# Attention with two feed-forward layers: the maxima's row as one DMA from SBUF into q's stack, and copies merged into fewer DMAs

## The chip, the cores and the metric

The kernel runs on one core of a Trainium2 chip. The metric is the device time of one execution in microseconds (us); smaller is better. TensorE (PE) does matrix products, VectorE (DVE), ScalarE (ACT) and GpSimd (POOL) the rest, SyncE (SP) issues nearly all DMAs.

## The reference

```python
def _attn_ref(q, k, v, g_q, g_k):              # q, k, v: (4, 12, 448, 64) float32
    q_n, k_n = (rmsnorm(q, g_q), rmsnorm(k, g_k))
    scores = scale * np.matmul(q_n, k_n.transpose(0, 1, 3, 2))
    scores = scores - np.max(scores, axis=-1, keepdims=True)
    attn = np.exp(scores)
    attn = attn / (np.sum(attn, axis=-1, keepdims=True) + 1e-09)
    return np.matmul(attn, v)
...
def _moe_ref(x, w_in, w_out, g_ln):            # x: (1792, 768), d_ff 1024
    h = x @ w_in
    solu = h * softmax(h)
    return (layer_norm(solu) * g_ln) @ w_out
...
def _moe2_ref(x, w_in, w_out):                 # d_ff 2048
    h = x @ w_in
    return ((h - np.tanh(h)) @ w_out)
```

The weights of the two layers come as 64-bit floats.

## The kernel before

Products are made more exact than one pass by splitting each operand into a high part and a rest; a product is then three passes (`three`, L174).

There are 4 batches of 12 heads. Heads are taken two at a time: 24 pairs. For each pair the kernel loads q and k (`load_qk`), normalises them (`norm`), transposes them on TensorE (`qk_trans`, twice), and splits them: ScalarE writes the high part, VectorE the rest. For every pair but the first, DMAs then copy these parts from a work tile (`wq`, `wk`) into stacks `Q` and `K`. A stack holds 128 partitions, so that one pass over it multiplies two parts at a time: for one head, the high part of q lies in 64 partitions and its rest in the other 64 (slot z = 0); slot z = 1 has the high part again, and in the other 64 partitions zeros, but for one partition, into which the row of that head's negated maxima is written. k's stack has ones opposite that row, so the pass subtracts the maximum of each query from its scores.

The row is made thus. `maxima` multiplies q's and k's high parts and VectorE takes the maximum of each query (`nm`, L355). `spread` transposes 4 columns of `nm` on TensorE (L362), ScalarE copies the 4x128 result to `nt` (L364), and two DMAs of SyncE's queue carry it: `nt` to a scratch tensor `m` in HBM (L367), and from there to the row in `Q` (L370). `weights` then makes the scores with the stacks (`sps`, L393), ScalarE the exponentials (`pf`, L404), and `pv` multiplies with v (`pvps`, L440 and L446). `load_v` fetches v: two DMAs of 3x128 rows, and one of 64 rows for the last 64 keys of each head (its tail).

The list `attn` gives each of these steps a slot; `spread` of a pair's first head comes 3 steps ahead of the first `weights` that needs its row, `spread` of its second head 2 steps ahead of the tail that needs it. After the first batch the steps are laid between those of the first feed-forward layer of the batch before (`overlap`: `moe_h`, `layer_norm`, `moe_x2`), and weights are fetched (L114), split (L153), saved to HBM (L157) and read again (L167) beside it. From 560 us on only the second layer is left.

The order on each engine isn't the code's: a planner lays the instructions by costs of its own when the program is built, and each engine then runs its list in order. SyncE's DMAs are one such list: an instruction that waits holds all behind it. Each DMA tells of its landing by one of eight semaphores, which the DMAs take in turn as the planner laid them, and it isn't issued before the one that had that semaphore last has landed.

Of the kernel before, what the change touches and what calls it, by code (L numbers as in the profile page):

```python
# [8 lines left out]
F32 = mybir.dt.float32  # L9
F32R = mybir.dt.float32r  # L10
# [8 lines left out]
def kernel(  # L19
# [14 lines left out]
    nc = tc.nc  # L34
    B, H, S, D = q.shape
# [7 lines left out]
    CP = S // 4  # L43
# [10 lines left out]
    NQ = 3  # L54
# [5 lines left out]
    dram = ctx.enter_context(tc.tile_pool(name="dram", bufs=1, space=bass.MemoryType.DRAM))  # L60
# [142 lines left out]
    def load_v(p):  # L203
        b, h = pair(p)
        if p in V32:

            t = vhl_t[p] = A["vh"].tile([128, 14, D], F32, tag="va", name="v32")
            tv = t.rearrange("p (a z) d -> p a z d", z=2)
            nc.gpsimd.memset(tv[:, :, 1], 1.0)
            for i in range(2):  # L210
                r = slice(64 * i, 64 * i + 64)
                nc.sync.dma_start(
                    out=tv[:, 3 * i:3 * i + 3, 0],
                    in_=v[b, h + i, 0:384, :].rearrange("(c p) d -> p c d", p=128),
                )
                nc.sync.dma_start(out=tv[r, 6, 0], in_=v[b, h + i, 384:448, :])
            return
        t = A["v"].tile([128, 7, D], F32, tag="v", name="vraw")
# [64 lines left out]
    def qk_trans(p, a):  # L283

        ps = ps_m.tile([128, 4, CP], F32, tag="m", name="qkps")
        for c in range(4):
            nc.tensor.transpose(ps[:, c], qn_t[p][:, a, c].rearrange("p h d -> p (h d)"), idf[:CP, :CP])
        if a == 0:
            w = Q[0][:, 0] if p == 0 else A["one"].tile([128, 2, 4, CP], F32R, tag="wq", name="wq")
            split(w[:, 0], w[:, 1], ps)  # L290
        else:
            w = K[0][:, 0] if p == 0 else A["one"].tile([128, 2, S], F32R, tag="wk", name="wk")
            hi, lo = (w[:, z].rearrange("r (p c) -> r p c", c=4) for z in range(2))
            pv = ps.rearrange("r c p -> r p c")
            nc.scalar.activation(out=hi, in_=pv, func=AF.Copy, scale=gam)
            nc.vector.scalar_tensor_tensor(
                out=lo, in0=pv, scalar=gam, in1=hi.bitcast(F32), op0=ALU.mult, op1=ALU.subtract,
            )
        w_t[p, a] = w
        if a == 0:  # L300
            for i in range(2):
                r = slice(64 * i, 64 * i + 64)
                f = 384 * (1 - i)
                copy(
                    nc.scalar, out=qd[p % 2][r, r],
                    in_=w[r, 0].rearrange("p c q -> p (c q)")[:, f:f + 64].bitcast(F32),
                )
        if p == 0:
            return

        t = Q[p % 2] if a == 0 else K[p % NQ]
        for i in range(2):
            r, o = slice(64 * i, 64 * i + 64), slice(64 - 64 * i, 128 - 64 * i)
# [18 lines left out]
    def fill_q(z):  # L332
        for i in range(2):
            o = slice(64 - 64 * i, 128 - 64 * i)
            constant(Q[z][o, i, 1].rearrange("p c q -> p (c q)"), o, zero)

    def maxima(p, c):


        if p not in nm_t:  # L340
            nm_t[p] = A["small"].tile([128, 7], F32, tag="nm", name="nm")
        ps = ps_x.tile([128, S], F32, tag="x", name="mps")
        i = c // 4
        r = slice(64 * i, 64 * i + 64)
        if c == 3:
            nc.tensor.matmul(ps, lhsT=qd[p % 2], rhs=w_t[p, 1][:, 0], start=True, stop=True)
        else:
            if p == 0:
                qh, kh = w_t[0, 0][r, 0], w_t[0, 1][r, 0]
            else:  # L350

                qh, kh = Q[p % 2][:, i, 0], K[p % NQ][:, i, 0]
            f = 128 * c if i == 0 else 128 * (c - 4) + 64
            nc.tensor.matmul(ps, lhsT=qh.rearrange("p c q -> p (c q)")[:, f:f + 128], rhs=kh, start=True, stop=True)  # L354
        nc.vector.tensor_reduce(out=nm_t[p][:, c:c + 1], in_=ps, axis=AX.X, op=ALU.max, negate=True)  # L355

    def spread(n):

        p, i = divmod(n, 2)
        o = 64 * i if p == 0 else 64 - 64 * i  # L360
        ps = ps_m.tile([128, 128], F32, tag="m", name="nmps")
        nc.tensor.transpose(ps[:4], nm_t[p][:, 3 * i:3 * i + 4], idf)  # L362
        nt = A["small"].tile([4, 128], F32R, tag="nt", name="nt")
        nc.scalar.activation(out=nt, in_=ps[:4], func=AF.Copy)  # L364
        t = (Q[0][o:o + 1, 1, i] if p == 0 else Q[p % 2][o:o + 1, i, 1]).rearrange("p c q -> p (c q)")
        m = dram.tile([4, 128], F32, name=f"m_{n}")
        nc.sync.dma_start(out=m, in_=nt.bitcast(F32))  # L367

        row = m.rearrange("(o c) q -> o (c q)", o=1)[:, 64 * i:64 * i + S]
        nc.sync.dma_start(out=t.bitcast(F32), in_=row)  # L370

    def weights(n, j):

# [2 lines left out]
        for i in ((1, 0) if j == 3 else (n % 2,)):  # L376
            r = slice(64 * i, 64 * i + 64)

            k0, m = ((384, 64), (320, 128))[i] if j == 3 else (128 * j, 128)
            if p == 0 and j == 3 and i == 0:  # L380

                p1, ps = ps, ps_x.tile([128, 4, CP], F32, tag="x", name="sps")
            o = ps[:m]
            if p == 0:
                qh, ql = w_t[0, 0][r, 0], w_t[0, 0][r, 1]
                kh, kl = w_t[0, 1][r, 0, k0:k0 + m], w_t[0, 1][r, 1, k0:k0 + m]
                nc.tensor.matmul(o, lhsT=kh, rhs=qh, start=True, stop=False)
                nc.tensor.matmul(o, lhsT=kh, rhs=ql, start=False, stop=False)
                nc.tensor.matmul(o, lhsT=kl, rhs=qh, start=False, stop=False)
                nc.tensor.matmul(o, lhsT=K[1][r, 1 - i, 1, :m], rhs=Q[0][r, 1, i], start=False, stop=True)  # L390
            else:
                for z in range(2):
                    nc.tensor.matmul(  # L393
                        o, lhsT=K[p % NQ][:, i, z, k0:k0 + m], rhs=Q[p % 2][:, i, z], start=(z == 0), stop=(z == 1)
                    )
        tail = "t" if j == 3 else ""
        x = A["pc" + tail if p in V32 else "pf"].tile(
# [315 lines left out]
    Q += [A["qt"].tile([128, 2, 2, 4, CP], F32R, tag=f"q{z}", name=f"q{z}") for z in range(2)]  # L713
    for z in range(2):
        o = slice(64 * z, 64 * z + 64)
        constant(Q[0][o, 1, z].rearrange("p c q -> p (c q)"), o, zero)
# [21 lines left out]
    b = 0  # L738
# [147 lines left out]
```

## Time and profile before

| | |
|---|---|
| time, median of 3 runs | 1158.94 us (1152.77 to 1166.38) |
| the profiled execution | 1158.77 us, of which the profile's span is 1156.9 us |
| TensorE busy | 1071.2 us (93%) |
| VectorE busy | 740.8 us (64%) |
| ScalarE busy | 525.3 us (45%) |
| DMA, share of 16 engines | 50.2% |

Busy time is that in which an engine executes; waits and DMA issues are not in it. A wait is put down to what ended it. The granted clock is TensorE's, as a share of 2.4 GHz: 0.50 is 1.2 GHz. Times inside the profile count from the span's start.

### The profile page before, as it was taken

Reading aid. Unit: us, or ns where it says so; the run is one execution under the profiler, and the core shown is the slowest. Engines: PE = TensorE matmul, PEld = TensorE weight load, DVE = VectorE, ACT = ScalarE, POOL = GpSimd, SP = SyncE. Lnnn points to the kernel's source line nnn. Section 1 sums busy time; section 2 is a strip of 40 time slices with the busy share of each in tenths; the row PEclk is TensorE's granted clock in tenths of the full one; section 3 lists DMA queues with packets and bytes.
Section 4 is the critical chain, followed back from the end, with each engine's and each line's share of the span. In section 5 each row is a group of like instructions: output and inputs, shape, how many; then the busy total and the mean of one; then the engine's idle time right before and its main releaser. Section 6 shows DMA issues by size and latency. Waiting matters only on the chain.

```text
span 1156.9 us, 19235 instructions
## 1 busy us (share of the span) xinstructions
PE 1071.2 (93%) x7152; PEld 948.0 (82%) x7152; DVE 740.8 (64%) x1331; ACT 525.3 (45%) x1064; POOL 263.5 (23%) x228
## 2 busy tenths in 40 slices
PE   5989988969887989997999999999999999999998
PEld 3545566646776779776998999999999999999998
DVE  8566677699798866654527045558575757667434
ACT  5466666688676767665226145312121212122111
POOL 3211122222312411111201031416050414142100
PEclk9999999998999899998999999999999999999999
DMA  6776688776997877765737534112121111211022
GB/s 173 204 220 170 169 220 230 217 216 208 266 290 239 251 207 212 194 210 165 247 110 227 181 125 137 60 52 74 38 74 38 56 56 46 65 37 56 1 83 110
DMA packets 112893, 171.53 MB, mean 148 GB/s; under 512 B 33328, under 2 KB 79136, under 8 KB 112800
## 3 DMA queue, kind: packets, MB, share of 16 engines
q1 hardware_dynamic: 112800, 170.30, 50.2%
q8 instruction: 57, 0.93, 0.3%
q14 instruction: 36, 0.29, 0.1%
HBM read 109.41 MB, written 29.20 MB: 120 GB/s over the span
## 4 chain that ended last, share of the span: by engine, by line
PE 66%; DMA 15%; DVE 9%; ACT 5%; issue 2%; SPq 1%; POOL 0%; DVEq 0%; ACTq 0%; POOLq 0%
PE ops L177 7%; PE h2ps L176 7%; PE h2ps L175 7%; PE h2ps L177 7%; PE ops L176 7%; PE ops L175 7%; PE pvps L440 5%; PE sps L393 3%; PE hps L175 2%; DMA w<-w_in 2%; DMA raw<-in_moe_w_out_dram 2%; PE x2ps L175 2%; PE hps L177 2%; PE hps L176 2%; PE x2ps L177 2%; PE x2ps L176 2%
## 5 line engine op out<-in xcount | busy, mean ns | idle before, releaser
L175 PE MATMUL ops<-w,gT 128*128 128x256 f32 x672 | 189.6, 282 | 1.4 <-ACT ob L818 0.8
L176 PE MATMUL h2ps<-x2s,w 128*128 128x256 f32 x672 | 189.5, 282 | 0.0
L176 PE MATMUL ops<-w,gT 128*128 128x256 f32 x672 | 189.4, 282 | 0.0
L177 PE MATMUL ops<-w,gT 128*128 128x256 f32 x672 | 188.9, 283 | 0.5 <-DVE gT L181 0.5
L177 PE MATMUL h2ps<-x2s,w 128*128 128x256 f32 x672 | 189.3, 282 | 0.0
L175 PE MATMUL h2ps<-x2s,w 128*128 128x256 f32 x672 | 189.3, 282 | 0.0
L154 POOL TENSOR_TENSOR w<-val,w 128x512 fp32r<-128x512 f32 x60 | 80.5, 1351 | 388.2 <-ACT w L153 382.1
L355 DVE TENSOR_REDUCE nm<-mps 128x1 f32<-128x448 f32 x168 | 103.1, 619 | 79.7 <-PE mps L354 73.7
L393 PE MATMUL sps<-q,k 128*128 128x448 f32 (+1 forms) x368 | 120.0, 415 | 23.0 <-DVE nm L355 9.4
L175 PEld LDWEIGHTS ops<-w,gT 128*128 128x128 f32 x672 | 127.7, 190 | 2.0 <-ACT ob L818 1.2
L176 PEld LDWEIGHTS ops<-w,gT 128*128 128x128 f32 x672 | 127.6, 190 | 0.0
L177 PEld LDWEIGHTS ops<-w,gT 128*128 128x128 f32 x672 | 126.8, 189 | 0.7 <-DVE gT L181 0.7
L175 PEld LDWEIGHTS h2ps<-x2s,w 128*128 128x128 f32 x672 | 127.2, 189 | 0.1
L177 PEld LDWEIGHTS h2ps<-x2s,w 128*128 128x128 f32 x672 | 127.0, 189 | 0.0
L176 PEld LDWEIGHTS h2ps<-x2s,w 128*128 128x128 f32 x672 | 126.9, 189 | 0.0
L798 DVE TENSOR_TENSOR th<-h2ps,th 128x512 f32<-128x512 f32 x56 | 38.6, 689 | 134.4 <-ACT th L797 134.4
L820 DVE TENSOR_TENSOR ob<-ops,ob 128x512 f32<-128x512 f32 x147 | 100.4, 687 | 24.5 <-PE ops L177 20.2
L797 ACT ACTIVATE th<-h2ps 128x512 f32<-128x512 f32 x56 | 33.4, 596 | 171.9 <-PE h2ps L177 171.3
L404 ACT ACTIVATE pf<-sps 128x448 f32<-128x448 f32 x167 | 87.6, 539 | 50.5 <-PE sps L393 42.5
L393 PEld LDWEIGHTS sps<-q,k 128*128 128x128 f32 (+1 forms) x368 | 63.5, 187 | 55.3 <-DVE nm L355 16.6
L175 PE MATMUL hps<-w,xs 128*128 128x256 f32 x336 | 97.4, 291 | 6.2 <-DMA w<-w_in 5.7
L176 PE MATMUL hps<-w,xs 128*128 128x256 f32 x336 | 95.9, 286 | 0.0
(139 smaller groups left out, 2371.2 us busy)
## 6 DMA issues: line engine op xcount, KB each, us to landing
w<-w_out SPq DMA_DIRECT2D x48, 512.0 KB
raw<-in_moe_w_in_dram SPq DMA_DIRECT2D x36, 512.0 KB
raw<-in_moe_w_out_dram SPq DMA_DIRECT2D x36, 512.0 KB
w<-w_in SPq DMA_DIRECT2D x36, 512.0 KB
q<-wq SPq DMA_DIRECT2D x138, 112.0 KB
k<-wk SPq DMA_DIRECT2D x46, 224.0 KB
w_in<-w SPq DMA_DIRECT2D x12, 512.0 KB
w_out<-w SPq DMA_DIRECT2D x12, 512.0 KB
```

The lines of the kernel that those rows point to most:

```text
L154: nc.gpsimd.tensor_tensor(out=w[:, 1], in0=x, in1=w[:, 0].bitcast(F32), op=ALU.subtract)
L175: nc.tensor.matmul(ps, lhsT=a[0], rhs=w[0], start=first, stop=False)
L176: nc.tensor.matmul(ps, lhsT=a[0], rhs=w[1], start=False, stop=False)
L177: nc.tensor.matmul(ps, lhsT=a[1], rhs=w[0], start=False, stop=last)
L355: nc.vector.tensor_reduce(out=nm_t[p][:, c:c + 1], in_=ps, axis=AX.X, op=ALU.max, negate=True)
L393: nc.tensor.matmul(o, lhsT=K[p % NQ][:, i, z, k0:k0 + m], rhs=Q[p % 2][:, i, z], start=(z == 0), stop=(z == 1))
L404: nc.scalar.activation(out=x, in_=ps, func=AF.Exp)
L440: nc.tensor.matmul(o, lhsT=w, rhs=x, start=first, stop=last)
L797: nc.scalar.activation(out=th, in_=ps, func=AF.Tanh)
L798: nc.vector.tensor_tensor(out=th, in0=ps, in1=th, op=ALU.subtract)
L820: nc.vector.tensor_tensor(out=o, in0=ps, in1=o, op=ALU.add)
```

## The change

The row no longer goes through HBM: one DMA, issued by ScalarE right behind its copy to `nt`, writes the 4x128 block into one partition of `Q`. The block is 64 elements longer than the row, so `Q` is laid out flat, with a gap of 64 that takes what is over. Because in that layout the two slots with q's high part lie side by side, the two DMAs that copied it become one, with a source that is read twice. The tails of v's two heads come in one DMA of 128 partitions instead of two of 64. At the start, four DMAs for the norms' factors become two; they and the layer norm's factor are issued by ScalarE.

```diff
+    QW, GAP = 4 * S + 64, 64
+    QO = {(0, 0): 0, (0, 1): S, (1, 1): 2 * S + GAP, (1, 0): 3 * S + GAP}
+    def qcols(t, o, p, i, z):
+        c = (2 + i) * S + GAP if p == 0 else QO[i, z]
+        return t[o, c:c + S]
...
     def load_v(p):
...
         for i in range(2):
             nc.sync.dma_start(
-                out=t[:, 3 * i:3 * i + 3],
+                out=chunks[:, 3 * i:3 * i + 3],
                 in_=v[b, h + i, 0:384, :].rearrange("(c p) d -> p c d", p=128),
             )
-            nc.sync.dma_start(out=t[64 * i:64 * i + 64, 6], in_=v[b, h + i, 384:448, :])
-        v_t[p] = t
+        nc.sync.dma_start(out=tails, in_=v[b, h:h + 2, 384:448, :])
...
     def qk_trans(p, a):
...
             if a == 0:
-                for z in range(2):
-                    nc.sync.dma_start(out=t[r, i, z].bitcast(F32), in_=w[r, 0].bitcast(F32))
-                nc.sync.dma_start(out=t[o, i, 0].bitcast(F32), in_=w[r, 1].bitcast(F32))
+                wf = w.rearrange("r z c q -> r z (c q)").bitcast(F32)
+                c = min(QO[i, 0], QO[i, 1])
+                nc.sync.dma_start(
+                    out=t[r, c:c + 2 * S].rearrange("r (z f) -> r z f", z=2).bitcast(F32),
+                    in_=wf[r, 0:1].to_broadcast([64, 2, S]),
+                )
+                nc.sync.dma_start(out=qcols(t, o, p, i, 0).bitcast(F32), in_=wf[r, 1])
...
     def spread(n):
...
         nc.scalar.activation(out=nt, in_=ps[:4], func=AF.Copy)
-        t = (Q[0][o:o + 1, 1, i] if p == 0 else Q[p % 2][o:o + 1, i, 1]).rearrange("p c q -> p (c q)")
-        m = dram.tile([4, 128], F32, name=f"m_{n}")
-        nc.sync.dma_start(out=m, in_=nt.bitcast(F32))
-        row = m.rearrange("(o c) q -> o (c q)", o=1)[:, 64 * i:64 * i + S]
-        nc.sync.dma_start(out=t.bitcast(F32), in_=row)
+        c = ((2 + i) * S + GAP if p == 0 else QO[i, 1]) - GAP * i
+        nc.scalar.dma_start(out=Q[p % 2][o:o + 1, c:c + S + GAP].bitcast(F32), in_=nt.bitcast(F32))
...
-    for z in range(2):
-        nc.sync.dma_start(out=gam[64 * z:64 * z + 64], in_=g_q.rearrange("(d o) -> d o", o=1))
-        nc.sync.dma_start(out=gam2[64 * z:64 * z + 64], in_=g_k.rearrange("(d o) -> d o", o=1))
-    nc.sync.dma_start(out=gln, in_=moe_g_ln.rearrange("(c p) -> p c", p=128))
+    for t, g in ((gam, g_q), (gam2, g_k)):
+        nc.scalar.dma_start(out=t, in_=g.rearrange("(o d) -> o d", o=1).to_broadcast([2, D]))
+    nc.scalar.dma_start(out=gln, in_=moe_g_ln.rearrange("(c p) -> p c", p=128))
```

SyncE's list in the first batch, where the copies of one pair into `k_164` and `q_166` stand. Before:

```order
L472 DMA xd<-xo 128x448
L320 DMA k_164<-wk 64x448
L319 DMA k_164<-wk 64x896
L370 DMA q_167<-m_709 1x448
L319 DMA k_164<-wk 64x896
L320 DMA k_164<-wk 64x448
L316 DMA q_166<-wq 64x448 x2
L317 DMA q_166<-wq 64x448
L316 DMA q_166<-wq 64x448 x2
L317 DMA q_166<-wq 64x448
L367 DMA m_804<-nt 4x128
```

The same copies on SyncE in the changed kernel, whose lines are some 8 higher:

```order
L480 DMA xd<-xo 128x448
L331 DMA k_164<-wk 64x448 x2
L330 DMA k_164<-wk 64x896 x2
L324 DMA q_166<-wq 64x2x448
L328 DMA q_166<-wq 64x448
L324 DMA q_166<-wq 64x2x448
L328 DMA q_166<-wq 64x448
```

The row's second DMA (L370) stood among the copies, and the next row's first (L367) behind them; now SyncE's list has neither, and six copies of q are four. In all SyncE issues 569 DMAs where it issued 740.

ScalarE's list at the same place, from one row's `nt` to the next. Before:

```order
L364 ACTIVATE nt<-nmps 4x128
L404 ACTIVATE pf<-sps 128x448
L295 ACTIVATE wk<-qkps,gam 128x448
L180 ACTIVATE wq<-qkps 128x448
L247 ACTIVATE sq<-qk 112x1024
L404 ACTIVATE pf<-sps 128x448
L74 ACTIVATE qd_160<-wq 64x64 x2
L128 ACTIVATE val<-raw_1497 128x512
L404 ACTIVATE pf<-sps 128x448
L364 ACTIVATE nt<-nmps 4x128
L404 ACTIVATE pf<-sps 128x448
```

The same on ScalarE in the changed kernel:

```order
L375 ACTIVATE nt<-nmps 4x128
L378 DMA q_166<-nt 1x4x128
L412 ACTIVATE pf<-sps 128x448
L302 ACTIVATE wk<-qkps,gam 128x448
L180 ACTIVATE wq<-qkps 128x448
L251 ACTIVATE sq<-qk 112x1024
L412 ACTIVATE pf<-sps 128x448
L74 ACTIVATE qd_160<-wq 64x64 x2
L412 ACTIVATE pf<-sps 128x448 x2
L375 ACTIVATE nt<-nmps 4x128
L378 DMA q_166<-nt 1x4x128
L466 ACTIVATE sx<-pvps,tiny 64x448
```

The row's DMA now stands right behind `nt`, ahead of the exponentials (`pf`) and of the copies of the transposed k and q (`wk`, `wq`); elsewhere in the list one to seven other instructions stand between.

## Rows read from the trace of the kernel before

**Rows 1.** Windows: stretch, length, busy us of PE, PEld, DVE, ACT, POOL, clock, DMA share, GB/s.

```profile
30.00:160.00 130.00, 117.91 (x456) 71.27 (x454) 79.94 (x155) 85.74 (x186) 26.89 (x30) 0.97 0.72 191
160.00:300.00 140.00, 119.12 (x593) 85.31 (x591) 117.78 (x232) 101.74 (x221) 36.91 (x35) 0.94 0.79 220
300.00:430.00 130.00, 109.83 (x581) 92.06 (x581) 105.93 (x213) 93.82 (x206) 31.14 (x29) 0.92 0.89 261
430.00:560.00 130.00, 116.99 (x696) 103.91 (x696) 78.35 (x145) 82.34 (x167) 22.30 (x23) 0.96 0.66 195
560.00:1157.00 597.00, 589.39 (x4792) 585.68 (x4791) 334.17 (x523) 146.55 (x250) 135.72 (x94) 1.00 0.27 86
```

**Rows 2.** Waits of PE in 0 to 560 us: total us, times, longest.

```profile
PE mps L354 <- DMA q<-wq: 9.8, 6, 3.2
PE sps L393 <- DVE nm L355: 9.4, 11, 1.7
PE sps L393 <- DMA q<-m: 8.6, 7, 3.5
...
PE mps L346 <- ACT qd L74: 4.7, 5, 1.9
PE sps L393 <- ACT pf L404: 4.6, 5, 1.8
...
PE mps L354 <- ACT pf L404: 2.8, 4, 1.1
PE sps L390 <- DMA q<-m: 1.9, 1, 1.9
```

**Rows 3.** Waits of SyncE's queue over the whole span.

```profile
SPq L370 <- DMA m<-nt: 31.1, 27, 4.2
SPq L367 <- ACT nt L364: 31.0, 19, 4.0
...
SPq L316 <- DMA raw<-in_moe_w_out_dram: 2.6, 2, 2.4
```

**Rows 4.** The page's chain that ended last, by engine.

```profile
PE 66%; DMA 15%; DVE 9%; ACT 5%; issue 2%; SPq 1%; POOL 0%; DVEq 0%; ACTq 0%; POOLq 0%
```

**Rows 5.** Timeline, 73 to 85 us: start, duration, instruction, idle before it and what ended it.

```profile
73.22 0.27 SPq L367 DMA_DIRECT2D m<-nt  x1
...
75.26 1.15 SPq L319 DMA_DIRECT2D k<-wk  x1
...
77.31 0.26 SPq L370 DMA_DIRECT2D q<-m  x1
...
79.46 2.12 SPq L316 DMA_DIRECT2D q<-wq  x2
...
81.02 0.67 PE L393 MATMUL sps<-q,k 128*128 128x448 f32 x2 [0.37 <-DMA q<-m]
...
84.92 0.44 PE L354 MATMUL mps<-k,q 128*128 128x448 f32 x1 [3.23 <-DMA q<-wq]
```

**Rows 6.** Single lines' DMA issues: ns least/median/most, first and last start.

```profile
L367 SPq DMA_DIRECT2D m<-nt x48: 265/293/674, 17.1 to 511.7; - x48
L370 SPq DMA_DIRECT2D q<-m x48: 218/242/440, 22.3 to 513.1; - x48
L316 SPq DMA_DIRECT2D q<-wq x92: 461/587/1524, 19.6 to 488.2; - x92
L718 SPq DMA_DIRECT2D gam<-in_g_q_dram x2: 568/582/596, 1.7 to 2.9; - x2
```

**Rows 7.** Windows with half the clock, first and last of six.

```profile
85.50:88.90 3.40, 2.82 (x6) 1.87 (x7) 1.15 (x2) 1.01 (x2) 0.00 (x0) 0.50 0.36 77
...
423.40:426.80 3.40, 3.40 (x11) 2.55 (x10) 1.25 (x3) 3.28 (x7) 0.00 (x0) 0.50 0.71 225
```

**Rows 8.** DMA queue of the page: packets, MB, share of 16 engines' span.

```profile
q1 hardware_dynamic: 112800, 170.30, 50.2%
```

More of the change, by code (lines that the diff above doesn't have):

```diff
@@ L209, in load_v @@
             nc.gpsimd.memset(tv[:, :, 1], 1.0)
[L210 to L218, printed above, removed]
+            chunks, tails = tv[:, 0:6, 0], tv[:, 6, 0]
+        else:
+            t = v_t[p] = A["v"].tile([128, 7, D], F32, tag="v", name="vraw")
+            chunks, tails = t[:, 0:6], t[:, 6]
         for i in range(2):
             nc.sync.dma_start(
-                out=t[:, 3 * i:3 * i + 3],
+                out=chunks[:, 3 * i:3 * i + 3],
                 in_=v[b, h + i, 0:384, :].rearrange("(c p) d -> p c d", p=128),
             )
-            nc.sync.dma_start(out=t[64 * i:64 * i + 64, 6], in_=v[b, h + i, 384:448, :])
-        v_t[p] = t
+        nc.sync.dma_start(out=tails, in_=v[b, h:h + 2, 384:448, :])
     def rsqrt(y, x, scale):
@@ L288, in qk_trans @@
         if a == 0:
-            w = Q[0][:, 0] if p == 0 else A["one"].tile([128, 2, 4, CP], F32R, tag="wq", name="wq")
+            w = (
+                Q[0][:, 0:2 * S].rearrange("r (z c q) -> r z c q", z=2, c=4) if p == 0
+                else A["one"].tile([128, 2, 4, CP], F32R, tag="wq", name="wq")
+            )
             split(w[:, 0], w[:, 1], ps)
@@ L314, in qk_trans @@
             if a == 0:
-                for z in range(2):
-                    nc.sync.dma_start(out=t[r, i, z].bitcast(F32), in_=w[r, 0].bitcast(F32))
-                nc.sync.dma_start(out=t[o, i, 0].bitcast(F32), in_=w[r, 1].bitcast(F32))
+                wf = w.rearrange("r z c q -> r z (c q)").bitcast(F32)
[3 more added lines that the diff above has]
+                    in_=wf[r, 0:1].to_broadcast([64, 2, S]),
+                )
+                nc.sync.dma_start(out=qcols(t, o, p, i, 0).bitcast(F32), in_=wf[r, 1])
             else:
@@ L334, in fill_q @@
             o = slice(64 - 64 * i, 128 - 64 * i)
-            constant(Q[z][o, i, 1].rearrange("p c q -> p (c q)"), o, zero)
+            constant(qcols(Q[z], o, 1, i, 1), o, zero)
     def maxima(p, c):
@@ L348, in maxima @@
             if p == 0:
-                qh, kh = w_t[0, 0][r, 0], w_t[0, 1][r, 0]
+                qh, kh = Q[0][r, 0:S], w_t[0, 1][r, 0]
             else:
-                qh, kh = Q[p % 2][:, i, 0], K[p % NQ][:, i, 0]
+                qh, kh = qcols(Q[p % 2], slice(0, 128), p, i, 0), K[p % NQ][:, i, 0]
             f = 128 * c if i == 0 else 128 * (c - 4) + 64
-            nc.tensor.matmul(ps, lhsT=qh.rearrange("p c q -> p (c q)")[:, f:f + 128], rhs=kh, start=True, stop=True)
+            nc.tensor.matmul(ps, lhsT=qh[:, f:f + 128], rhs=kh, start=True, stop=True)
         nc.vector.tensor_reduce(out=nm_t[p][:, c:c + 1], in_=ps, axis=AX.X, op=ALU.max, negate=True)
@@ L389, in weights @@
                 nc.tensor.matmul(o, lhsT=kl, rhs=qh, start=False, stop=False)
-                nc.tensor.matmul(o, lhsT=K[1][r, 1 - i, 1, :m], rhs=Q[0][r, 1, i], start=False, stop=True)
+                nc.tensor.matmul(o, lhsT=K[1][r, 1 - i, 1, :m], rhs=qcols(Q[0], r, 0, i, 1), start=False, stop=True)
             else:
@@ L393, in weights @@
                     nc.tensor.matmul(
-                        o, lhsT=K[p % NQ][:, i, z, k0:k0 + m], rhs=Q[p % 2][:, i, z], start=(z == 0), stop=(z == 1)
+                        o, lhsT=K[p % NQ][:, i, z, k0:k0 + m], rhs=qcols(Q[p % 2], slice(0, 128), p, i, z), start=(z == 0), stop=(z == 1)
                     )
@@ L712 @@
     K += [A["qt"].tile([128, 2, 2, S], F32R, tag=f"k{z}", name=f"k{z}") for z in range(NQ)]
-    Q += [A["qt"].tile([128, 2, 2, 4, CP], F32R, tag=f"q{z}", name=f"q{z}") for z in range(2)]
+    Q += [A["qt"].tile([128, QW], F32R, tag=f"q{z}", name=f"q{z}") for z in range(2)]
     for z in range(2):
         o = slice(64 * z, 64 * z + 64)
-        constant(Q[0][o, 1, z].rearrange("p c q -> p (c q)"), o, zero)
-    for z in range(2):
-        nc.sync.dma_start(out=gam[64 * z:64 * z + 64], in_=g_q.rearrange("(d o) -> d o", o=1))
-        nc.sync.dma_start(out=gam2[64 * z:64 * z + 64], in_=g_k.rearrange("(d o) -> d o", o=1))
-    nc.sync.dma_start(out=gln, in_=moe_g_ln.rearrange("(c p) -> p c", p=128))
+        constant(qcols(Q[0], o, 0, z, 1), o, zero)
+    for t, g in ((gam, g_q), (gam2, g_k)):
+        nc.scalar.dma_start(out=t, in_=g.rearrange("(o d) -> o d", o=1).to_broadcast([2, D]))
+    nc.scalar.dma_start(out=gln, in_=moe_g_ln.rearrange("(c p) -> p c", p=128))
     nc.vector.scalar_tensor_tensor(out=gam, in0=gam, scalar=scale, in1=gam2, op0=ALU.mult, op1=ALU.mult)
```

## Prediction

> **What bounds the kernel now.** First the windows, to see which stretches the change can reach. From 560 us on TensorE is busy for 589 of 597 us at full clock, and nothing of attention is left: that half can't change by more than when it starts. Before 560 us TensorE is busy for 84 to 91% of each stretch, at a mean clock of 0.92 to 0.97, and no other engine is full: VectorE, the next, has 118 of 140 us and 106 of 130 us in the two densest [rows 1]. So the first 560 us are a pipeline that loses time by waits, and what matters is which wait ends last at TensorE.
>
> Second, TensorE's waits. Two kinds that the change touches stand high: for the row of maxima in `Q` (L370's DMA) 8.6 + 1.9 us, for the copies of q 9.8 us; together 20.3 us in 14 waits. The rest shown is VectorE's maxima and ScalarE [rows 2].
>
> Third, why they come late: SyncE's queue. It waits 31.1 us for the first leg of the row to land in HBM before it may issue the second, and 31.0 us for ScalarE's `nt` [rows 3]; everything behind stands. One place shows both effects: the first leg is issued at 73.22 us, the second only at 77.31; the copies of q start at 79.46, and TensorE waits at 81.0 us for the row and then 3.23 us for the copies, to 84.92 [rows 5].
>
> **The change part by part.** The sum is made against the profiled execution's 1158.77 us, 0.2 us from the median.
>
> The row. The first leg (issue and flight, 4.1 us at that place [rows 5]) goes; one flight stays. Its duration isn't in the trace, since no DMA runs from SBUF to one partition: the nearest is the second leg, 3.7 us to the wait's end at that place [rows 5], and it may be less, as HBM is not read. Also gone is the time in which the first leg stood in SyncE's queue behind the copies. The longest wait for a row is 3.5 us [rows 2], less than the 4.1 us removed, so I take all of the 10.5 us; the other end is none of it, if the new flight were as long as both legs.
>
> The copies of q. For each pair SyncE is rid of two legs of 0.27 us and 0.24 us for each of two rows, of two copies of 0.59 us [rows 6], and of the standstill before the second leg, 0.9 us at the place shown (from 76.41, when L319 is through, to 77.31) [rows 5]. Of the 3.23 us that TensorE waited there, some 0.9 + 0.25 + 2 x 0.59 = 2.3 us go. I take three quarters of the 9.8 us, 7.4; ends 0 and 9.8.
>
> Together 17.9 of the 20.3 us.
>
> The clock. In the first 560 us there are stretches of 3.4 us at half clock (0.50), each behind a stretch in which TensorE stood idle; six of them come right after waits for the row or the copies [rows 7]. Busy at half clock loses 1.7 us each, 10.2 us for six; by the same share of waits removed (17.9 of 20.3), 9.0 us. Ends 0 and 10.2.
>
> What is late next. 26.9 us is what TensorE would gain if all else were ready. It isn't: VectorE ends 11 waits of the scores already, and ScalarE 14 more [rows 2], and VectorE at 81 to 84% busy [rows 1] has less room than TensorE's gain suggests. No row gives the share that is kept; the ends are 0 and all. I take 0.65, as these other waits are short (under 2 us each) and spread: 17.5 us.
>
> ScalarE's cost. It issues 48 DMAs in line with its work. No DMA of ScalarE is in the trace; SyncE's issues last 0.24 to 0.59 us [rows 6]. I take 0.6, the longer kind, because this one has a shape of three dimensions and must first see `nt` finished: 29 us. ScalarE is busy for 364 of 530 us between 30 and 560 us [rows 1], so it has room, but the exponentials and the copies that queue behind the DMA are what TensorE waits for. The share that reaches the end: ScalarE holds 5% of the chain, 58 us, for 525 us of busy time [rows 4], 11%, or 3.2 us; if a third of it came through, 10 us. I take 5. Below nothing isn't excluded only if the planner's new order helps; I give that no value.
>
> At nothing: the start. Five issues of 0.58 us [rows 6] leave SyncE, 2.9 us, and three join ScalarE, beside its table load; the first pair's load stands ahead of them on SyncE's list, and TensorE's first product needs no more than that. If the cover were gone it would cost ScalarE's three issues, 1.8 us. The merged tails of v save 24 issues on SyncE and are wanted a slot later; they come back as a rival.
>
> The sum: -17.5 + 5 = -12.5 us, 1146.3: **1146 us**.
>
> **The rivals.**
>
> *VectorE takes the gain.* The waits vanish where they are named and come back as waits for the maxima. For it: the scores wait 9.4 us for VectorE's maxima already, and it is over 80% busy from 160 to 430 us [rows 1, 2]. Against it: before 160 us and after 430 it is busy for about 60% [rows 1], and the place shown lies there. If a quarter to half of the 26.9 us is kept, that is 7 to 13 less 5: 1150 to 1157 us.
>
> *ScalarE is held at its own DMA: slower.* The row's DMA must wait, besides for `nt`, for the DMA that had its semaphore before, which stands some eight places earlier in the plan and mostly on SyncE's list. On SyncE such a wait held only copies; on ScalarE it holds exponentials, so SyncE's delays reach the engine that feeds TensorE. For it: SyncE itself stood 1.3 us a time before a copy until a weight's fetch had landed, and waited for its own row's flight 31.1 us in all [rows 3]; between 300 and 430 us DMAs are 89% busy [rows 1], so earlier ones land late. Against it: SyncE has 171 fewer issues, so eight places earlier lies further back. The price: a hold of x us at each of 48 rows on top of 0.6, of which a third (dense) comes through: 16 x (0.6 + x). It cancels the 17.5 us at x = 0.5; at 1.5 us, as SyncE's waits are, it costs 34 us: 1158.8 - 17.5 + 34 = 1175. With half the rows so held it is 1163.
>
> *The tails crowd two DMA queues.* The merged tail reads a source whose outer dimension is 2. If the DMA is shared out by that, its 128 pieces of 256 bytes go to two of the 16 engines, 64 each, where 16 that share them alike have 8 each. The mean packet takes 0.502 x 16 x 1156.9 / 112800 = 82 ns for 1.5 KB [rows 8]; a 256-byte one is between that and its share by bytes, 14 ns. So 56 more packets are 0.8 to 4.6 us per pair on those two. From 300 to 430 us, with some six pairs, that is 5 to 28 us, where the engines have 11% of 130 us, 14 us, free [rows 1]: nothing to 14 us late, so 1146 to 1160. What speaks for the low end is that v is wanted late.
>
> This is a rule of the Trainium skill (DMA: Bandwidth & Descriptors, Rules for kernel authors): a DMA whose outermost dimension has fewer than 16 entries runs on no more than that many engines. No row here shows which engine took a packet; by the rule the crowding would happen and the time be that of this rival, and without it 1146.
>
> **How the numbers follow.** About 1% (11.6 us) is what a measurement of this kernel can tell from no change, so 1147.4 and 1170.5 are the bounds. My forecast, 1134 to 1150: 0.50, of which 0.42 lies under 1147.4. More than the sum, with nearly everything kept and weights fetched earlier by a freer SyncE, 1122 to 1134: 0.06. VectorE takes it: 0.24. ScalarE held: 0.15, counted as slower. Tails: 0.05. Faster 0.48, the same 0.08 + 0.24 + 0.05 = 0.37, slower 0.15. The range from 1128 to 1166 leaves out half of the 0.06 and most of the 0.15.
>
> **What would show it.** Right: no wait of TensorE for the row above 1 us, waits for q's copies under 4 us in all, the mean clock between 30 and 560 us up from 0.95 by about 0.02, and the last attention product some 12 us earlier. The cost: ScalarE's queue shows 48 issues of about 0.6 us, and its waits before them are short. Wrong by the first rival: waits for `nm` grow by what the others lose. By the second: ScalarE's queue waits at the row's DMA for other DMAs by a microsecond or more, and waits for `pf` and `qd` grow at TensorE. By the third: loads land later between 300 and 430 us. I would also be wrong if the planner's new order opened a wait at a place with no name here, since the lists of VectorE and ScalarE are laid anew over the whole first half.

## The result: slower by 0.8%, with the waits for the row gone

| | before | after |
|---|---|---|
| median of 20 runs each | 1159.1 us | 1167.6 us (1161.4 to 1172.7) |
| ratio, 95% interval | | 1.008 [1.006, 1.010] |
| the profile's span | 1156.9 us | 1161.2 us |
| mean granted clock of the profiled execution | 0.976 | 0.964 |

The forecast was 1146 us, faster. These are the rows of after that answer to those of before. Windows, with the columns of [rows 1]:

```profile
30.00:160.00 130.00, 120.53 (x505) 74.85 (x505) 93.02 (x173) 92.61 (x201) 31.50 (x34) 0.96 0.80 210
160.00:300.00 140.00, 109.41 (x513) 78.77 (x514) 114.77 (x237) 100.03 (x222) 31.93 (x30) 0.87 0.80 227
300.00:430.00 130.00, 111.85 (x615) 95.45 (x614) 96.28 (x195) 91.35 (x197) 32.84 (x32) 0.93 0.83 234
430.00:560.00 130.00, 114.99 (x667) 102.49 (x667) 75.62 (x142) 80.58 (x162) 19.17 (x20) 0.93 0.67 186
560.00:1157.00 597.00, 592.31 (x4821) 589.39 (x4819) 335.46 (x525) 148.61 (x254) 137.15 (x95) 1.00 0.27 87
```

TensorE's instruction counts show where the time goes. From 30 to 160 us it issues 505 where before had 456. From 160 to 300 us it issues 513 where before had 593, at a clock of 0.87 instead of 0.94 [rows 1], and the lead is gone. The second layer then only starts later. The early lead isn't the change's own: f3 below, with after's instructions in before's order, has 457 in the same stretch:

```profile
30.00:160.00 130.00, 115.57 (x457) 69.95 (x457) 83.63 (x160) 86.28 (x188) 28.67 (x32) 0.92 0.72 189
```

The clock of this first stretch can't be compared either. The trace's records of the clock begin at 51.4 us in before and at 29.3 us in after, and what lies ahead of the first record counts as 1.00; the products say otherwise, as h1 shows below.

Waits of TensorE from 0 to 560 us in after, as [rows 2]:

```profile
PE mps L365 <- DMA q<-wq: 25.8, 10, 4.4
PE qkps L291 <- DVE nr L239: 10.6, 1, 10.6
PE sps L401 <- ACT pf L412: 7.3, 8, 2.3
...
PE mps L365 <- ACT pf L412: 6.1, 6, 2.2
...
PE sps L401 <- DVE nm L366: 0.8, 3, 0.3
...
PE sps L401 <- DMA q<-nt: 0.2, 1, 0.2
```

The row, 8.6 + 1.9 us before [rows 2], is down to 0.2. The copies of q went from 9.8 to 25.8. SyncE's queue no longer waits for `nt` or for the first leg [rows 3], but it stands elsewhere; its waits over the whole span:

```profile
...
SPq L225 <- ACT va L283: 36.4, 7, 10.1
...
SPq L546 <- DMA xd<-xo: 14.0, 7, 4.6
```

It waits 36.4 us for a buffer of v (10.4 in before), and 14.0 us for a store that it has itself issued (1.6 in before). Single lines of after, as [rows 6]: ScalarE's row DMA, the merged copies of q, and VectorE's product of the two factors with what it waited for:

```profile
L378 ACTq DMA_DIRECT2D q<-nt x48: 580/581/682, 20.3 to 519.9; - x48
...
L324 SPq DMA_DIRECT2D q<-wq x46: 602/625/1647, 23.0 to 491.1; - x46
...
L728 DVE SCALAR_TENSOR_TENSOR gam<-gam,gam x1: 159/159/159, 7.8 to 7.8; 128x1 f32<-128x1 f32 x1
...
  DMA gam<-in_g_k_dram: 3.2, 1
```

The row's DMA takes ScalarE 0.58 us, as forecast (0.6). At 43 of the 48 rows it goes out within 0.1 us of what stands ahead of it. At five it is held until an earlier DMA with the same semaphore has landed, 7.2 us in all; the longest hold, 3.8 us, ends with the landing of a store of x2d. ScalarE's timeline there:

```profile
372.29 0.25 ACT L375 ACTIVATE nt<-nmps 4x128 fp32r<-4x128 f32 x1
376.33 0.58 ACTq L378 DMA_DIRECT2D q<-nt  x1
376.95 0.31 ACT L235 ACTIVATE nr<-ss,eps 112x16 f32<-112x16 f32 x1 [4.42 <-DMA x2d<-x]
```

At the start VectorE stands 3.2 us for the factors, ahead of the first pair's sums on its list. TensorE's first product waits until 10.6 us; in e1 and e2 below, which load the factors as before, until 7.5 and 7.4.

One wait for q's copies in after and what follows it, in the timeline (columns as [rows 5]) and in a window (as [rows 7]):

```profile
170.44 1.07 SPq L328 DMA_DIRECT2D q<-wq  x1
...
174.88 0.89 SPq L328 DMA_DIRECT2D q<-wq  x1
...
176.14 0.71 PE L365 MATMUL mps<-k,q 128*128 128x448 f32 x1 [4.17 <-DMA q<-wq]
```

```profile
176.10:179.50 3.40, 3.36 (x7) 2.40 (x8) 2.00 (x4) 1.34 (x3) 1.27 (x1) 0.50 0.93 282
```

4.17 us idle, then 3.4 us at half clock. The product waits for the copies issued at 169.59 and 170.44 us; the one at 174.88 is the other head's. The chain that ended last can't be set beside [rows 4]: in after it is followed back only to 266.6 us, and its shares add up to 76%.

### The profile page after: what moved, and what is told of

It is laid out like the page before. It is cut to its first block, busy times and chain, and to the rows that moved or that the text cites. A ratio compares the mean times of both kernels' runs of the same rounds, so it can differ in the third digit from the quotient of the medians.

```text
span 1161.2 us, 18987 instructions
## 1 busy us (share of the span) xinstructions
PE 1065.0 (92%) x7152; PEld 949.4 (82%) x7152; DVE 740.1 (64%) x1331; ACT 528.4 (46%) x1064; POOL 262.0 (23%) x228
## 4 chain that ended last, share of the span: by engine, by line
PE 59%; DMA 11%; DVE 4%; ACT 1%; issue 1%; SPq 0%; POOL 0%; ACTq 0%; DVEq 0%; POOLq 0%
PE h2ps L176 7%; PE h2ps L175 7%; PE ops L177 7%; PE h2ps L177 7%; PE ops L176 7%; PE ops L175 7%; DMA q<-wq 3%; PE x2ps L175 3%; PE x2ps L176 3%; PE x2ps L177 3%; DMA w<-w_in 2%; PE pvps L448 2%; PE hps L175 2%; PE hps L177 2%; PE hps L176 2%; PE sps L401 2%
## 5 line engine op out<-in xcount | busy, mean ns | idle before, releaser
L401 PE MATMUL sps<-q,k 128*128 128x448 f32 (+1 forms) x368 | 116.2, 414 | 9.7 <-ACT pf L412 7.3
L365 PE MATMUL mps<-k,q 128*128 128x448 f32 (+1 forms) x144 | 71.3, 503 | 34.5 <-DMA q<-wq 25.8
```

The source lines that it names most:

```text
L365: nc.tensor.matmul(ps, lhsT=qh[:, f:f + 128], rhs=kh, start=True, stop=True)
L401: nc.tensor.matmul(o, lhsT=K[p % NQ][:, i, z, k0:k0 + m], rhs=qcols(Q[p % 2], slice(0, 128), p, i, z), start=(z == 0), stop=(z == 1))
```

## The experiments

All ratios are to the kernel before, on the same chip. "Clock" is the profiled execution's mean granted clock, with the time ahead of its first record counted as 1.00.

| run | lists laid by | ratio, 95% interval | clock |
|---|---|---|---|
| before | planner | 1 | 0.976 |
| after | planner | 1.008 [1.006, 1.010] | 0.964 |
| e1 factors as before | planner | 1.0055 [1.0025, 1.008] | 0.959 |
| e2 row alone | planner | 0.992 [0.989, 0.996] | 0.973 |
| e3 merges alone | planner | 1.013 [1.009, 1.016] | 0.959 |
| e4 row on SyncE | planner | 1.010 [1.006, 1.0145] | 0.965 |
| e5 row, q merged | planner | 1.010 [1.006, 1.013] | 0.959 |
| e6 row, tails merged | planner | 0.997 [0.994, 1.0005] | 0.975 |
| e7 row, one start DMA moved | planner | 1.010 [1.0075, 1.013] | 0.962 |
| e8 row, copies turned | planner | 1.0085 [1.0055, 1.0115] | 0.961 |
| f1 = e7's instructions | e2's | 0.992 [0.9885, 0.995] | 0.972 |
| f2 = e2's instructions | before's | 0.996 [0.993, 0.999] | 0.974 |
| f3 = after's instructions | before's | 0.998 [0.995, 1.001] | 0.972 |
| f4 = after's instructions | e2's | 0.990 [0.985, 0.995] | 0.971 |
| g1 = e2's instructions | after's | 1.012 [1.007, 1.016] | 0.964 |
| g2 = after, four edges | planner | 1.0035 [1.000, 1.007] | 0.965 |
| g3 = e2, five edges | planner | 0.997 [0.994, 0.9995] | 0.976 |
| g4 = e1's instructions | e2's | 0.9855 [0.981, 0.990] | 0.976 |
| h1 = e7, two DMAs moved | e7's | 1.000 [0.9965, 1.003] | 0.972 |
| h2 = before's instructions | e2's | 1.034 [1.031, 1.037] | 0.963 |

### Parts undone, one at a time

My first theory: each part has a price of its own, and the merged copies, landing late, eat what the row gives. The rival (B): what counts is how the planner happens to lay the lists.

e1, against after:

```diff
-    for t, g in ((gam, g_q), (gam2, g_k)):
-        nc.scalar.dma_start(out=t, in_=g.rearrange("(o d) -> o d", o=1).to_broadcast([2, D]))
-    nc.scalar.dma_start(out=gln, ...)
+    for z in range(2):
+        nc.sync.dma_start(out=gam[64 * z:64 * z + 64], ...)
+        nc.sync.dma_start(out=gam2[64 * z:64 * z + 64], ...)
+    nc.sync.dma_start(out=gln, ...)
```

> The changed kernel with the three small factors loaded as before (five DMAs of SyncE, four of 64 partitions each). Theory A (each part has its own price): TensorE's first product comes back from 10.6 to 7.5 us and the time falls by 3 us, to 1164 or 1165, about 1.005 of before; the loss between 220 and 300 us stays. Rival B (what counts is how the planner happens to lay the lists, and any edit lays them anew): the first product comes back too, but the end is anywhere from 1150 to 1175, and the stretch from 220 to 300 us looks different.

1.0055: TensorE's first product waits 7.5 us again, but the interval reaches after's, and the profiled execution is longer than after's.

e2, against before, is the `spread` and the flat stack of the change alone.

> Only the row: one DMA of ScalarE's queue from SBUF into the flat stack; copies of q, tails of v and the factors as before. Theory A1 (the merged copies and tails give the gain back, by landing later): 1145 to 1150, waits for q's copies under 12 us. Theory A2 (the row itself gives it back, as ScalarE runs ahead into the weights' conversion from 220 to 300 us): 1158 to 1163 with that loss still there. Rival B (the plan's luck): no fixed relation, anywhere from 1145 to 1170.

0.992: the row alone is faster, as A1 said; waits for q's copies are 9.2 us.

e3, against before, has the two merges alone:

```diff
-                for z in range(2):
-                    nc.sync.dma_start(out=t[r, i, z]..., in_=w[r, 0]...)
+                nc.sync.dma_start(out=t[r, i]..., in_=w[r, 0:1].to_broadcast([64, 2, S]))
...
-            nc.sync.dma_start(out=t[64 * i:64 * i + 64, 6], in_=v[b, h + i, 384:448, :])
+        nc.sync.dma_start(out=tails, in_=v[b, h:h + 2, 384:448, :])
```

> The kernel before with only the merges of q's high copies and of v's tails; the row still goes through HBM in two DMAs of SyncE, the factors as before. Theory A1 (merges land later and cost): 1163 to 1168, waits of TensorE for q's copies above 20 us where they were 9.8. Theory A2 (the row gives it back): 1156 to 1160, waits for q's copies as before. Rival B (the plan's luck): anywhere from 1150 to 1170.

1.013, or 1177 us, more than A1 allowed, and waits for q's copies were 9.9 us, not above 20. Rival B's 1150 to 1170 doesn't hold it either. The merges seemed guilty, though not in the way I had named.

e4, against after, is `nc.sync` for `nc.scalar` in `spread`.

> The changed kernel with the row's single DMA on SyncE's queue in place of ScalarE's; all else equal, and the lists of TensorE, VectorE and ScalarE almost the same as in the changed kernel. If ScalarE's 48 issues of 0.58 us cost 5 us of the end, as forecast, and SyncE's queue costs little: 1162 or 1163. If SyncE's queue holds the row (waits for nt, copies behind them): waits for the row come back at TensorE by 5 us or more and the time is 1170 or more. If ScalarE's issues lie wholly beside other work and SyncE has room: 1167 to 1168, no change.

1.010, not to be told from after. The row's DMA now waits 25.3 us for `nt` on SyncE, yet TensorE's waits for the row are only 2.0 us (0.2 in after). What ScalarE's 28 us of issues cost isn't shown by this: the lists differ more than I had expected, at least 161 of VectorE's 1331 instructions stand elsewhere than in after.

e5 and e6 are e2 with one merge each, the diffs as above.

> The row by ScalarE's DMA plus the merged copies of q's high part; tails of v and factors as before. The row alone measured 0.992 of before, row and both merges 1.0055. Theory A (the merge has a price, as q's copies land later): 1.002 to 1.006 of before, TensorE's waits for q's copies near 20 us, where the row alone has 9.2. If the tails carry the price: 0.990 to 0.995 and waits for q's copies near 9. Rival B (the plan's luck): no fixed relation.

> The row by ScalarE's DMA plus the merged tails of v; copies of q and factors as before. Theory A (q's merged copies carry the price): 0.990 to 0.995 of before. Theory A' (the tails carry it, by crowding the copies on the DMA engines): 1.002 to 1.006, with q's copies landing later though they are not merged. Rival B (the plan's luck): no fixed relation.

1.010 and 0.997, neither in a range of theory A or A'. Had I stopped here, I would have written that q's merged copies cost 1.8%. Two controls speak against it.

### Controls: edits that should cost nothing

e7 is e2 with one 4 KB DMA of the start on another queue, e8 is e2 with the heads' copies in the other order:

```diff
-    nc.sync.dma_start(out=gln, in_=moe_g_ln.rearrange("(c p) -> p c", p=128))
+    nc.scalar.dma_start(out=gln, in_=moe_g_ln.rearrange("(c p) -> p c", p=128))
```

```diff
-        for i in range(2):
+        for i in (1, 0):
```

> A control for the plan: the row alone, and one single DMA of the start (the layer norm's factor, 4 KB, not used in the first 200 us) on ScalarE's queue in place of SyncE's. By itself it can cost 0.6 us of ScalarE's time at the start. Yet the planner lays 434 of TensorE's 7050, 332 of VectorE's 1333 and 220 of ScalarE's 1100 instructions in another place, about as many as for the merged copies (477, 386, 305). Theory A (parts have their own prices): 0.989 to 0.996 of before, as the row alone. Rival B (the plan's luck decides): more than 0.5% away from the row alone, 0.987 or less, or 0.997 or more.

> A second control for the plan: the row alone, with the copies into the stacks issued for the second head first and then for the first; the same DMAs, as many, to the same places. The planner lays 497 of TensorE's, 374 of VectorE's and 364 of ScalarE's instructions in another place. The pair's first maxima need the first head, so a cost of its own is at most the two or three issues of 0.55 us that now stand ahead of it in the pairs where TensorE waits for q's copies (4 such waits in the row alone): up to 5 us. Theory A: 0.990 to 0.997 of before. Rival B (the plan's luck): outside of that.

1.010 and 1.0085: both 1.6 to 1.8% above e2, as much as any part, where e7 could cost 0.6 us of its own and e8 5. Theory A falls: edits of next to nothing move the kernel further than the change did.

### The lists held

To hold a list, the kernel carries a table of each engine's order and draws an ordering edge (no wait, only the order in the engine's list) from each instruction to the next:

```diff
+    for name, text in ORDER.items():
+        row = [lists[name][at] for at in places(text)]
+        for a, b in zip(row, row[1:]):
+            tc.add_manual_dep(b, a.name, DependencyInfo(NoSync, DATA), reason="order")
```

Instructions that the list's owner doesn't have stand beside their nearest kin: a merged DMA where the first of the two stood, the row's DMA behind `nt`, the factors at the head. In f2, f3 and h2 GpSimd's list stays the planner's. No run holds a kernel to its own lists; that the edges by themselves cost nothing rests on f1 below, which is as fast as e2 without edges.

> The control e7_gln_queue again (the layer norm's factor on ScalarE's queue), but with every engine's list held to that of the row alone by ordering edges, so that the planner can lay nothing anew. The row alone measured 0.992 of before, the control 1.010. Rival B (the lists decide): back to 0.989 to 0.996. Theory A (the moved DMA itself costs): stays at 1.007 to 1.013.

0.992, where the same instructions in the planner's own lists gave 1.010. The 1.8% is the lists'.

> The row alone, but TensorE's, VectorE's and ScalarE's lists held to those of the kernel before (the row's DMA right behind nt on ScalarE, the two legs taken out of SyncE's list, nothing else moved but six of GpSimd's fills). It measures the row without the planner. My forecast's terms for the row (10.5 us of waits, the queue's standstill for q's copies 2.3 us, half of the clock, kept share 0.65, ScalarE's cost 5): 0.988 to 0.994 of before. If the row has no worth of its own and the row alone's 0.992 was luck of the lists: 0.998 to 1.002. If ScalarE's 48 issues cost more than the waits gave: 1.003 or more.

> The whole change, with the lists of TensorE, VectorE and ScalarE held to those of the kernel before; a merged copy of q stands where the first of the two stood, a merged tail where the first tail stood, the factors' three DMAs at the head of ScalarE's list. Rival B (the lists that the planner laid lost the time, not the parts): 0.985 to 0.996 of before. Theory A (the merges and the factors' loads cost by themselves): 1.004 to 1.010, as the changed kernel (1.008), with TensorE's waits for q's copies near 20 us.

0.996 and 0.998, neither in a range that I had written down: in the lists of before, the row is worth 0.4%, and the whole change 0.2%, which can't be told from nothing. The waits of f2 show where part of the rest went:

```profile
PE sps L399 <- DVE nm L364: 11.9, 13, 2.2
PE hps L175 <- DMA w<-w_in: 9.0, 6, 2.3
PE mps L363 <- DMA q<-wq: 8.5, 6, 2.9
PE mps L355 <- ACT qd L74: 7.6, 8, 2.0
...
PE mps L363 <- DVE nm L364: 4.9, 5, 1.7
```

The row is no longer among the larger waits. In its place the scores wait 11.9 us for the maxima (9.4 before), the products of the maxima 4.9 (2.8), and `qd` costs 7.6 (4.7 before) [rows 2]. In f3, with the merges, TensorE waits 11.1 us for q's copies, more than in f2 and in before.

> The whole change, with all lists held to those of the row alone (merged DMAs where the first of each stood). Against the row alone (0.992) it differs by the merges and the factors alone, with no list laid anew. If the merges cost nothing and the start its 3 us: 0.992 to 0.997 of before. If the merged copies and tails land too late by themselves: 1.004 or more, with waits for q's copies well above the row alone's 9.2 us.

> The mirror of f4_all_in_row_lists: the row alone (copies, tails and factors as before) held to the lists that the planner laid for the changed kernel. If the lists lose the time: 1.001 to 1.008 of before, with the loss between 220 and 300 us in it. If the merges lose it: 0.989 to 0.996, as the row alone had (0.992).

0.990 and 1.012, each a little beyond the range for the lists. The whole change in e2's lists is as fast as e2; e2 in after's lists is as slow as after. The merges have no price that shows in the time, though TensorE's waits for q's copies rise from e2's 9.2 us to 15.5 in f4; which lists are laid decides. One window of after and of f4, the same instructions in other lists, shows where; first after, then f4:

```profile
260.00:300.00 40.00, 29.40 (x151) 23.11 (x150) 35.15 (x78) 30.19 (x70) 9.54 (x9) 0.82 0.69 202
```

```profile
260.00:300.00 40.00, 36.42 (x223) 29.97 (x221) 35.87 (x71) 31.89 (x75) 9.66 (x9) 0.96 0.83 252
```

VectorE is as busy in both (35 of 40 us); TensorE issues 151 instructions in one and 223 in the other, at a clock of 0.82 against 0.96. So VectorE does other things first.

### Two places in the lists

VectorE's list between the 108th and the 109th maximum of after, conversions of the output weights (`val`, `w`) and the maxima alone:

```
L366 TENSOR_REDUCE nm<-mps 128x1
...
L137 SCALAR_TENSOR_TENSOR val<-raw_3388,val 128x512
L148 SCALAR_TENSOR_TENSOR w_3371<-val,gln,w_3371 128x128 x4
L140 SCALAR_TENSOR_TENSOR val<-raw_3388,val 128x512
...
L137 SCALAR_TENSOR_TENSOR val<-raw_3407,val 128x512
L140 SCALAR_TENSOR_TENSOR val<-raw_3407,val 128x512
...
L148 SCALAR_TENSOR_TENSOR w_3390<-val,gln,w_3390 128x128 x4
...
L366 TENSOR_REDUCE nm<-mps 128x1
```

Parts of three conversions stand there. In f4's list, `w_3390` comes behind the 113th maximum:

```
L366 TENSOR_REDUCE nm<-mps 128x1
L148 SCALAR_TENSOR_TENSOR w_3390<-val,gln,w_3390 128x128 x4
```

g2 holds the ninth to twelfth conversion of after back to where they stand in e2, and leaves the lists alone up to VectorE's 448th instruction. g3 squeezes five in e2 (its edges run from a maximum to the end of a conversion).

```diff
+    for i, n in {8: 111, 9: 112, 10: 117, 11: 123}.items():
+        tc.add_manual_dep(first_of_conversion[i], maximum[n - 1].name, DependencyInfo(NoSync, DATA), reason="order")
```

> The changed kernel with four ordering edges: the ninth to twelfth conversion of the output weights may not start on VectorE ahead of the 111th, 112th, 117th and 123rd row maximum, as they stand in the row alone's list. All lists are the changed kernel's up to the 448th instruction of VectorE; from there 86 of VectorE's and 64 of TensorE's instructions stand elsewhere. Theory S (the squeezed conversions cost): of the 20 us lost between 220 and 300 us 8 to 15 come back: 0.995 to 1.001 of before. Rival (the loss is elsewhere in the lists, in q's copies or in ScalarE's list): 1.005 to 1.011.

> The row alone with the converse edges: five row maxima may not stand on VectorE ahead of the end of the sixth to tenth conversion, so that these are squeezed between the 99th and the 113th maximum, as in the changed kernel. Lists are the row alone's up to the 418th instruction of VectorE. Theory S: the row alone's 0.992 rises to 0.998 to 1.006. Rival: 0.989 to 0.995, no change.

1.0035 and 0.997: about 0.45% in each direction, of the 1.8% that lie between the two sets of lists. Each interval overlaps that of its origin, and both effects are smaller than the theory's ranges. The traces don't bear the theory out. From the 108th maximum to the 109th it is 19.0 us in after and 12.2 in f4, but 19.4 in g2: conversions still stand there, and the edges moved others. So g2 doesn't test the place shown, and TensorE issues 150 instructions in its window, as after's 151:

```profile
260.00:300.00 40.00, 31.45 (x150) 23.08 (x149) 29.53 (x67) 31.31 (x70) 9.63 (x9) 0.80 0.69 197
```

In g3 the same step goes from e2's 12.4 to 16.2 us. Windows of e2 and then of g3:

```profile
260.00:300.00 40.00, 33.73 (x208) 27.52 (x207) 35.27 (x70) 30.42 (x73) 5.31 (x5) 0.95 0.82 235
```

```profile
260.00:300.00 40.00, 31.52 (x180) 25.57 (x180) 31.80 (x65) 29.75 (x68) 9.14 (x9) 0.91 0.83 237
```

But g3's execution was late before its edges act. Up to VectorE's 417th instruction its lists are e2's, and yet TensorE's 400th instruction starts at 131.6 us in e2 and at 136.6 in g3. So two executions of one list can lie 5 us apart by then, and a window of one execution each can't price the squeeze.

The second place is SyncE's list in e7. h1 holds e7's lists and moves two DMAs behind four:

```diff
-L205 DMA qk<-in_k_dram 112x2x256
-L206 DMA qk<-in_q_dram 112x2x256
 L326 DMA q_167<-wq 64x448
 L325 DMA q_167<-wq 64x448 x2
 L326 DMA q_167<-wq 64x448
+L205 DMA qk<-in_k_dram 112x2x256
+L206 DMA qk<-in_q_dram 112x2x256
```

> The control e7_gln_queue held to its own lists (1.010 of before), but on SyncE's list the loads of a later pair's k and q, which stood ahead of the last four of the first six copies of q, now stand behind them. Nothing else differs on any engine. In the control TensorE waited 3.2 us for these copies at 27 us and ran at half clock for 24 us before 60 us. Theory (a wait costs through the clock): that wait falls under 1 us, half clock before 60 us falls to 14 us or less, and the time by 4 to 9 us, to 1.002 to 1.007 of before. Rival (a wait costs only itself, or the two loads are missed later): 1.007 to 1.013.

1.000 instead of 1.010, more than I expected, and outside both ranges. The timeline of e7, and of h1:

```profile
24.77 0.53 SPq L205 DMA_DIRECT2D qk<-in_k_dram  x1
25.34 0.76 SPq L206 DMA_DIRECT2D qk<-in_q_dram  x1
26.21 0.52 SPq L326 DMA_DIRECT2D q<-wq  x1
...
30.29 0.71 PE L363 MATMUL mps<-k,q 128*128 128x448 f32 x1 [3.20 <-DMA q<-wq]
```

```profile
24.53 0.54 SPq L326 DMA_DIRECT2D q<-wq  x1
...
27.17 0.53 SPq L205 DMA_DIRECT2D qk<-in_k_dram  x1
...
28.04 0.71 PE L363 MATMUL mps<-k,q 128*128 128x448 f32 x1 [0.74 <-issue]
```

And the window behind it, e7, then h1:

```profile
20.00:60.00 40.00, 36.71 (x90) 19.83 (x89) 23.69 (x42) 19.94 (x43) 16.64 (x13) 0.70 0.61 160
```

```profile
20.00:60.00 40.00, 38.67 (x101) 21.33 (x101) 26.46 (x48) 22.44 (x47) 16.64 (x13) 1.00 0.68 182
```

One copy issued 1.7 us earlier takes a wait of 3.2 us down to 0.7. The two clocks, 0.70 and 1.00, say less than they seem to: the records begin at 26.5 us in e7 and at 49.9 us in h1, and what lies ahead counts as 1.00. The same product takes as long in h1, without a record, as in e7 at a recorded 0.50; in e2, at a recorded 1.00, it takes 0.36 us. First e7, then h1, then e2:

```profile
31.84 0.57 PE L395 MATMUL sps<-q,k 64*128 64x448 f32 x1
```

```profile
29.60 0.57 PE L395 MATMUL sps<-q,k 64*128 64x448 f32 x1
```

```profile
27.62 0.36 PE L395 MATMUL sps<-q,k 64*128 64x448 f32 x1
```

So h1 didn't run this stretch at full clock, and the theory that the wait costs through the clock isn't shown. TensorE's list is the same in both, and each instruction can be compared: h1 is 2.2 us ahead at 47 us, 2.3 at 287, 4.1 at 370, 8.7 at 415 and 8.4 at the end. The place itself gives some 2 us, about the wait; most of the rest arises between 320 and 415 us (616 instructions of TensorE against 566 from 300 to 430 us), and why isn't shown.

### What is left

> The changed kernel with the factors loaded as before, held to the row alone's lists: the version that should be the fastest. If the factors' start costs 2 to 3 us: 0.986 to 0.990 of before (f4_all_in_row_lists, with the factors' new loads, measured 0.990). If nothing: 0.990 to 0.992.

0.9855 [0.981, 0.990], a median of 1144.8 us beside 1160.5: row and merges, the factors loaded as before, in e2's lists. It beats both kernels.

> The kernel before, row through HBM, held to the row alone's lists; on SyncE's list the row's two legs stand, one DMA apart, at the place in the plan where ScalarE issued the row. The row alone in these lists measured 0.992, the changed kernel 0.990. If the lists alone are the gain: 0.990 to 0.994 here too. If the row is worth what it was in the old lists (0.4%): 0.994 to 0.999. If the two legs, laid by hand, hold SyncE's queue: above 1.000.

1.034, so it doesn't tell what e2's lists are worth without the row. SyncE's waits show why:

```profile
SPq L370 <- DMA m<-nt: 84.5, 43, 5.0
```

Laid so close, the second leg holds SyncE's queue for 84.5 us, where the planner's own places cost 31.1 [rows 3].

## Why the prediction was wrong

**The step that failed** is the one on what the planner does: "Below nothing isn't excluded only if the planner's new order helps; I give that no value", and, as the last sentence, that I would be wrong if the new order opened a wait at a place with no name. The first stands in ScalarE's term and is the only place of the sum that speaks of it. I priced the edits as if the lists would stay but for the named instructions. They don't: 0.990 against 1.008 for the same instructions in two sets of lists (f4, after), 0.992 against 1.010 for another (f1, e7). That term is 1.8% wide, some 21 us, more than the whole sum of 12.5. But the sum was too large by itself: in before's lists the whole change gives 0.998 (f3), 1156 us on my scale, 10 us above the forecast; the other 12 of after's 1168 are the lists'.

**The row** was right as a wait in after: 10.5 us went to 0.2. In e2's lists 5 to 8 us of waits for the row are left (6.8 in f4, 5.3 in g4, 7.6 in e2), and these kernels are the fastest: the wait that I priced isn't what sets the time.

**The copies of q**: I took 7.4 of 9.8 us. In the old lists 9.8 became 8.5 (f2), and 11.1 with the merges (f3). At 170.44 us in after, the copy's issue is over at 171.5 and TensorE goes on at 176.1: the flight is what lasts, and SyncE's freed slots don't shorten it. (The row's first leg takes 0.29 us at the median [rows 6], not the 0.27 that I took for its issue; it changes nothing.) Over all copies of q's rest the flight, from the end of the issue to the last step of the semaphore, is 2.6 us at the median in before and 4.0 in after.

**The kept share**, 0.65, was mis-sized too. With the lists held the row gave 0.4%, some 4 us (1 to 8 by the interval), and the whole change 2. That is the first rival by its time: f2's ratio is 1154 us on my scale and f3's 1156, inside its 1150 to 1157. Its place is borne out only in part: all waits of TensorE for `nm` together went from 19.1 us to 23.8 in f2, 4.7 of the 11.8 us that the row and the copies lost, and to 19.4 in f3.

**ScalarE's cost**: 0.58 us an issue was right; whether 5 us of it reach the end isn't shown, as e4's lists differ. The second rival's mechanism is there, and its price isn't: five of 48 rows were held, twice for more than a microsecond, 7.2 us in all, where it needed 0.5 us at every row, 24 us. One of its signs came too: TensorE's waits for `pf` shown went from 7.4 us [rows 2] to 13.4 in after. What share of the 21 us this is stays open.

**The start** at nothing, 1.8 us at most, was wrong: TensorE's first product comes 3.1 us later in after, as VectorE's product of the factors stands ahead of the first pair. I bounded it by ScalarE's issues and forgot who waits for the landing. About half is the lists': the first product waits until 9.0 us in g1 (after's lists, factors as before), 9.2 in f4 (e2's lists, new loads) and 7.4 in g4 (e2's lists, factors as before). Between f4 and g4 the intervals overlap, so the timing alone doesn't show it.

**The third rival**, the tails on two DMA engines: in held lists the merges cost nothing that shows in the time. f4 and g4, with them, are 0.990 and 0.9855, f1 without them 0.992; e6 with the tails alone is 0.997, in lists of its own. The crowding itself is there: the semaphore of a merged tail moves in three steps, one at the end of the issue and two later, where that of an unmerged tail moves in sixteen, and its flight is 3.0 us at the median in after, 1.7 for an unmerged one in e2. By the same section of the Trainium skill (DMA: Bandwidth & Descriptors, Rules for kernel authors), two transfers to disjoint halves of the partitions are better made one; no time here shows a gain by it. Its rule on the outermost dimension agrees with the steps of the semaphore.

**The clock** was to rise by 0.02 between 30 and 560 us. From 160 us on, where both have records, it went from 0.94 to 0.87, from 0.92 to 0.93 and from 0.96 to 0.93. The 0.97 that I read for 30 to 160 us in before [rows 1] counts 21 us without a record as full. With all time ahead of the first record at 0.50, as the products there suggest, the mean of the execution would be 0.954 in before and 0.950 in after, by my estimate, instead of 0.976 and 0.964. Across the profiled executions every kernel that isn't slower than before has 0.971 to 0.976, and every slower one 0.959 to 0.965; but over all its executions g3 (0.997) has a median of 0.967, as after has. So the clock alone doesn't split the fast kernels from the slow.

Still open: the 1.8% between after's lists and e2's. The loss shows between 260 and 300 us; which place in the lists makes it isn't shown.

## What to carry to other kernels

Where a planner lays the lists, one small edit is one draw: hold the lists by ordering edges, or time two or three edits that should cost nothing, before a per cent is put down to a part. Give that draw its own width in a forecast (here 2%), next to the sum of the edits. And when a good draw turns up, keep it: e2's lists with the change's instructions are the fastest kernel here. A window of one execution each prices nothing that is smaller than the 5 us by which e2 and g3 differ ahead of their first difference.

## What the runs showed of the hardware that I had not expected

The clock of TensorE has no record at first: the records begin at 26.6 us in e2 and at 50.1 us in g3, with the same lists up to there. Until then a product takes as long as at a recorded 0.50 (0.57 us against 0.36), and a mean that counts this time as 1.00 misleads. Besides, two DMAs of 128 four-byte pieces each, issued at 0.7 and 1.9 us by ScalarE, had landed at 4.6 and 7.7 us, whereas the four of 64 pieces that SyncE issued from 1.7 to 3.5 us in before had all landed by 5.9.
